# A Fourier mixing layer with a gated MLP: the first stage's four engines ordered by one written list

## The chip, the cores and the metric

The kernel runs on one core of one Trainium2 chip. The core has a matrix engine (TensorE, PE in the profile), a vector engine (VectorE, DVE), a scalar engine (ScalarE, ACT), a general engine (GpSimd, POOL), and DMA queues, most of them issued by SyncE (SP). SBUF is the working memory with 128 partitions; PSUM is the accumulator memory that TensorE writes, with 8 banks of 512 fp32 numbers a partition. POOL here works on SBUF only. Each engine runs its own instruction list in order, and waits where data of another engine is missing. The metric is device time of one execution in microseconds (us); lower is better.

## The reference

```
h  = x + irfft2(rfft2(layernorm(x)) * (w_r + 1j * w_i))
n  = layernorm(h)
h2 = h + (gelu(n @ w_gate) * (n @ w_up)) @ w_down
```

x is 2048 rows of 512 numbers; the filter w is 2048 x 257; the MLP is 1376 wide. All is fp32. layernorm takes mean and variance over the 512 numbers of a row, with 1e-5 added to the variance, and has no weights.

## The kernel before

The rows are cut into 16 blocks b of 128 rows (row 16 p + b lies in partition p), 512 columns each. The Fourier transforms are matrix products with tables. The work runs in stages: a first stage (the transform over the rows within a partition index, block by block), a second stage (the transform over the columns, the filter and the way back, 16 steps t), a third that returns to rows, adds the residual and normalises again, and then the MLP, most of the time. The change touches the first stage only (lines 213 to 400).

For each block b the first stage does this. The letters are those of the written list in the change, and the prediction uses them for both kernels.

- `s`, `g`: bn_stats on DVE over 512 numbers (`stats`, L220) and its merge to mean and variance in `mv` (`merge`, L223). For blocks 5, 7, 9, 11 and 13 ScalarE takes these instead: `m`, the mean by a scaled copy with an accumulator (`mean`, L228), and `q`, the variance by a square with an accumulator (`square`, L233).
- `r`: a reciprocal root of variance + eps on ScalarE (`root`, L240), and beside it on DVE variance + eps into a PSUM tile `tmp` (L241). Blocks 0 and 1 each alone, then pairs (2, 3), (4, 5) and so on.
- `n`: one Newton step on DVE that sharpens the root (`newton`, L246 to L248): three operations, each of which takes one operand from `rs` in SBUF and one from `tmp` in PSUM.
- `c`: the block's 128 x 128 transform matrix times this root on ScalarE (`scale`, L256), from `mfs` into `ms`, so that layernorm's division needs no pass over x.
- `f`: POOL's fold of x: a difference (L262) and a sum (L263) of the two halves of the columns, into `pn`; 256 numbers each for the single blocks 0, 1, 14 and 15, 512 for a pair.
- `v`: the second fold on DVE (`fold2`, L277): the difference of the two halves of `pn`, into `uv`. Both inputs lie in SBUF.
- `u`: the sum that goes with it (L275), into `us`. Before the change it is made for block 15 only.
- `a`, `b`: TensorE's products of the block (`transform`, L288). An fp32 product is two matmul instructions in the trace. Quarters c = 0 and 1 of the output (`a`) take two products each from `pn`, or one each from `us` where `u` was made; quarters 2 and 3 (`b`) take one each from `uv`. So a block is 12 instructions, or 8 with `u`.
- `k`: the copy of the block's PSUM bank (bank b mod 7) on ScalarE into `ts` (`keep`, L293).

The second stage's first matmul (`over_d`, L416) reads `ts` of all 16 blocks.

What sets the order: DVE's instructions of the first stage are issued as the calls stand in the code (`manual_schedule` with DVE alone); the orders of PE, ACT and POOL are made by the framework's planner. In the second and the later stages all four engines follow lists written by hand (`SECOND`, `FIRST`). SP issues the loads in the order of the code: x of blocks 0, 1, 2-3, 4-5, the matrices of blocks 2-7, more x, then tables, the first weights, the filter. `lasts` is the last `fold2`: POOL's work on the first MLP weights (`load_gu(0)`, L138) waits for it (`behind`), to leave DVE the port that both use. ScalarE's halving of `wh` is put behind the last copy, `kept`.

Of the kernel before, what the change touches and what calls it, by code (L numbers as in the profile page):

```python
# [20 lines left out]
P = 128  # L21
NB = 16
# [3 lines left out]
EPS = 1e-5  # L26
# [31 lines left out]
def kernel(  # L58
# [103 lines left out]
    with (  # L162
# [54 lines left out]
        def stats(b):  # L217

            bns[b] = w1.tile([P, 6], F32, name="bn", bufs=4)
            dve.bn_stats(bns[b], gh[:, b])  # L220

        def merge(b):
            dve.bn_aggr(mv[:, b], bns[b])  # L223
# [10 lines left out]


        tmp = ps[:, 7].rearrange("p (b k) -> p b k", b=NB)

        def root(b, n):

            act.activation(rs[:, b : b + n], mv[:, b : b + n, 1], AF.Abs_reciprocal_sqrt, bias=eps)  # L240
            dve.tensor_scalar(tmp[:, b : b + n, 0], mv[:, b : b + n, 1], EPS, None, op0=ALU.add)  # L241

        def newton(b, n):

            r, (ve, t) = rs[:, b : b + n], (tmp[:, b : b + n, k] for k in range(2))
            dve.scalar_tensor_tensor(t, r, -0.5, ve, op0=ALU.mult, op1=ALU.mult)  # L246
            dve.tensor_tensor(t, t, r, op=ALU.mult)
            dve.scalar_tensor_tensor(r, t, 1.5, r, op0=ALU.add, op1=ALU.mult)  # L248

        mss, parts = {}, {}  # L250

        def scale(*bs):

            for b in bs:
                mss[b] = w1.tile([P, 2, P // 2], F32, name="ms", bufs=6)
                act.activation(mss[b], mfs[:, b], AF.Copy, scale=rs[:, b : b + 1])  # L256

        def fold(b, n):
            xv = gh[:, b : b + n].rearrange("p b (e n) -> p b e n", e=2)
            pn = w1.tile([P, 2, 2, 2, P], F32, name="pn", bufs=7)[:, :n]  # L260
            pv = pn.rearrange("p b e h n -> p b e (h n)")
            pool.tensor_tensor(pv[:, :, 1], xv[:, :, 0], xv[:, :, 1], op=ALU.subtract)  # L262
            pool.tensor_tensor(pv[:, :, 0], xv[:, :, 0], xv[:, :, 1], op=ALU.add)  # L263
            for i in range(n):
                parts[b + i] = [[pn[:, i, 0, 0], pn[:, i, 0, 1]], [pn[:, i, 1, 0], pn[:, i, 1, 1]]]
            return pn

        def fold2(b, n, sums=False):

            nonlocal lasts  # L270
            pn = pns[b]
            uv = w1.tile([P, 2, 2, P], F32, name="uv", bufs=3)[:, :n]
            if sums:
                us = w1.tile([P, 2, P], F32, name="us", bufs=1)
                dve.tensor_tensor(us, pn[:, 0, :, 0], pn[:, 0, :, 1], op=ALU.add)  # L275
                parts[b] = [[us[:, 0]], [us[:, 1]]]
            lasts = dve.tensor_tensor(uv, pn[:, :, :, 0], pn[:, :, :, 1], op=ALU.subtract)  # L277
            for i in range(n):
                parts[b + i] += [[uv[:, i, 0]], [uv[:, i, 1]]]

        def transform(b):

            pt = ps[:, b % 7].rearrange("p (c n) -> p c n", c=4)
            for c in range(4):

                mc = mss[b][:, :: -1 if c in (1, 2) else 1]
                for z, o in enumerate(parts[b][c]):
                    pe.matmul(pt[:, c], o, mc, start=(z == 0), stop=(z == len(parts[b][c]) - 1))  # L288

        def keep(b):  # L290
            pt = ps[:, b % 7].rearrange("p (c n) -> p c n", c=4)
            tv = ts[:, :, :, :, b].rearrange("p t c g k -> p t (c g) k")
            return act.activation(tv, pt.rearrange("p c (g t k) -> p t (c g) k", g=2, k=4), AF.Copy)  # L293

        pns = {b: fold(b, n) for b, n in GROUPS}
        with tc.manual_schedule(engines={mybir.EngineType.DVE}):

            stats(0)
            merge(0)
            root(0, 1)  # L300
            stats(1)
            newton(0, 1)
            merge(1)
            root(1, 1)
            fold2(0, 1)
            scale(0)
            newton(1, 1)
            fold2(1, 1)
            mean(5)
            transform(0)  # L310
            keep(0)
            scale(1)
            transform(1)
            keep(1)
            stats(2)
            merge(2)
            stats(3)
            merge(3)
            root(2, 2)
            square(5)  # L320
            stats(4)
            newton(2, 2)
            scale(2, 3)
            merge(4)
            root(4, 2)
            fold2(2, 2)
            transform(2)
            keep(2)
            transform(3)
            keep(3)  # L330
            mean(7)
            square(7)
            stats(6)
            newton(4, 2)
            scale(4, 5)
            merge(6)
            root(6, 2)
            fold2(4, 2)
            transform(4)
            keep(4)  # L340
            transform(5)
            keep(5)
            mean(9)
            square(9)
            stats(8)
            newton(6, 2)
            scale(6, 7)
            merge(8)
            root(8, 2)
            fold2(6, 2)  # L350
            transform(6)
            keep(6)
            transform(7)
            keep(7)
            mean(11)
            square(11)
            stats(10)
            newton(8, 2)
            scale(8, 9)
            merge(10)  # L360
            root(10, 2)
            fold2(8, 2)
            transform(8)
            keep(8)
            transform(9)
            keep(9)
            mean(13)
            square(13)
            stats(12)
            newton(10, 2)  # L370
            scale(10, 11)
            merge(12)
            root(12, 2)
            fold2(10, 2)
            transform(10)
            keep(10)
            transform(11)
            keep(11)
            stats(14)
            newton(12, 2)  # L380
            scale(12, 13)
            merge(14)
            stats(15)
            merge(15)
            root(14, 2)
            fold2(12, 2)
            transform(12)
            keep(12)
            transform(13)
            keep(13)  # L390
            newton(14, 2)
            scale(14, 15)
            fold2(14, 1)
            transform(14)
            keep(14)
            fold2(15, 1, sums=True)
            transform(15)
# [63 lines left out]
        def patch_w(t):  # L461
            act.activation(wts[t][:, :, :, 0:129:128], wh[:, t], AF.Copy)

        et = mybir.EngineType
# [486 lines left out]
        next(begun_tiles[n])  # L951

    do["g2P0"] = lambda: step(2)
    et = mybir.EngineType
# [216 lines left out]
```

## Time and profile before

| | us |
|---|---|
| median of 3 runs (454.14 to 454.22) | 454.15 |
| the profiled execution | 454.05 |
| its span, first to last instruction | 452.3 |
| PE busy | 437.8 (97%) |
| POOL busy | 276.5 (61%) |
| DVE busy | 277.1 (61%) |
| ACT busy | 205.6 (45%) |
| first matmul of the first stage | at 7.28 |
| last copy of the first stage ends | at 32.26 |
| first matmul of the second stage | at 32.30 |

The span runs from the first to the last instruction of the profiled execution; 1.75 us of its time lie outside. A row of the timeline gives start (us), duration (us), engine, line, operation, what it writes and reads, the shape, and in brackets the idle time before it and what ended it. "x8" means eight instructions merged into one row. A row of the chain gives start, length and the engine and line that the end of the kernel hung on. A row of the windows gives a stretch, its length, and busy time (with instruction count) of each engine in the order PE, PE's weight loads, DVE, ACT, POOL, then the granted TensorE clock, the DMA share and GB/s. Instructions of one engine overlap a little: a duration can be longer than the distance to the next start.

### The profile page before, as it was taken

The page shows a single profiled execution, that of the slowest core. Times are in us where ns is not written, and L with a number is a line of the kernel's source. Part 1 is how long each engine was busy: PE and PEld are TensorE (multiplying, and loading weights), DVE is VectorE, ACT ScalarE, POOL GpSimd, SP SyncE. Part 2 cuts the span into 40 slices and gives each one's busy share as a digit, 9 for nine tenths or more (in the row PEclk, how much of TensorE's full clock was granted, in tenths as well). Part 3 has the DMA queues.
Part 4 walks back from the last instruction along what each step waited for, and adds up shares of the span by engine and source line. Part 5 has one row for each costly group of instructions (what it writes and reads, how often), then busy time and mean ns, then how long its engine had stood idle before and what let it go on. Part 6 is the DMA issues. An engine that isn't in the chain of part 4 may idle for free.

```text
span 452.3 us, 6433 instructions
## 1 busy us (share of the span) xinstructions
PE 437.8 (97%) x2289; PEld 371.1 (82%) x2289; DVE 277.1 (61%) x514; ACT 205.6 (45%) x433; POOL 276.5 (61%) x306
## 2 busy tenths in 40 slices
PE   3999999999999999999999999999999999999996
PEld 3999999798878777877888888888888888888875
DVE  5957895797574766358735578266555345635453
ACT  4979785688731242033332765252243034303420
POOL 6986896878859578748662543165566636653210
PEclk9999999999999999999999999999999999999999
DMA  8994805200032022112210213121022102210013
GB/s 288 390 400 147 278 13 179 100 23 1 25 116 93 26 69 93 48 46 71 70 48 23 70 48 116 49 91 46 26 70 71 46 24 71 70 46 25 23 70 118
DMA packets 21168, 41.05 MB, mean 91 GB/s; under 512 B 2064, under 2 KB 7696, under 8 KB 21008
## 3 DMA queue, kind: packets, MB, share of 16 engines
q1 hardware_dynamic: 20992, 40.51, 26.3%
q8 instruction: 18, 0.29, 0.3%
q10 hardware_dynamic: 144, 0.13, 0.1%
q14 instruction: 14, 0.11, 0.1%
HBM read 36.44 MB, written 4.19 MB: 90 GB/s over the span
## 4 chain that ended last, share of the span: by engine, by line
PE 90%; DVE 3%; ACT 2%; DMA 2%; POOL 1%; issue 1%; SPq 0%; POOLq 0%; DVEq 0%
PE ps L756 26%; PE ps L100 15%; PE ps L102 14%; PE ps L101 14%; PE ps L288 4%; PE ps L416 3%; PE ps L427 3%; PE ps L454 3%; PE ps L524 3%; PE ps L862 1%; PE ps L971 1%; DMA gh<-in_x 1%; POOL gu L156 1%; PE ps L563 1%; DMA raw<-in_wgu 1%; PE ps L557 1%
## 5 line engine op out<-in xcount | busy, mean ns | idle before, releaser
L100 PE MATMUL ps<-cb,gu 128*128 128x512 f32 (+1 forms) x336 | 127.9, 381 | 2.0 <-ACT s L660 1.6
L756 PE MATMUL ps<-wd,a 128*128 128x512 f32 (+1 forms) x537 | 125.9, 388 | 0.2 <-DVE gh L759 0.2
L102 PE MATMUL ps<-cb,gu 128*128 128x512 f32 (+1 forms) x336 | 125.0, 372 | 0.0
L101 PE MATMUL ps<-cb,gu 128*128 128x512 f32 (+1 forms) x336 | 124.9, 372 | 0.0
L756 PEld LDWEIGHTS ps<-wd,a 128*128 128x128 f32 x537 | 99.4, 188 | 21.9 <-DVE gh L972 1.0
L156 POOL TENSOR_TENSOR gu<-raw,gu 128x768 fp32r<-128x768 f32 (+1 forms) x54 | 78.3, 1479 | 39.6 <-DVE gu L153 33.4
L660 ACT ACTIVATE s<-ps 128x512 f32<-128x512 f32 (+1 forms) x72 | 40.4, 560 | 133.8 <-PE ps L102 133.5
L100 PEld LDWEIGHTS ps<-cb,gu 128*128 128x128 f32 x336 | 63.3, 188 | 14.9 <-ACT s L660 2.2
L101 PEld LDWEIGHTS ps<-cb,gu 128*128 128x128 f32 x336 | 63.3, 188 | 11.7 <-issue 1.0
L102 PEld LDWEIGHTS ps<-cb,gu 128*128 128x128 f32 x336 | 63.3, 188 | 11.0
L762 DVE TENSOR_TENSOR gh<-ps,gh 128x512 f32<-128x512 f32 x48 | 33.1, 691 | 53.7 <-PE ps L756 53.5
L505 POOL TENSOR_TENSOR wd<-wdr,wd 128x512 fp32r<-128x512 f32 x22 | 28.4, 1291 | 51.3 <-ACT wd L503 51.2
L669 DVE TENSOR_TENSOR ps<-ps,s 128x512 f32<-128x512 f32 (+1 forms) x48 | 31.0, 650 | 24.4 <-PE ps L102 22.2
L675 ACT ACTIVATE a<-ps 128x512 fp32r<-128x512 f32 (+1 forms) x48 | 26.9, 561 | 39.0 <-DVE ps L669 38.6
L682 DVE TENSOR_TENSOR a<-ps,a 128x512 fp32r<-128x512 f32 (+1 forms) x48 | 30.8, 641 | 11.5 <-ACT a L675 9.8
L663 DVE TENSOR_TENSOR s<-ps,s 128x512 f32<-128x512 f32 (+1 forms) x48 | 30.9, 643 | 10.6 <-PE ps L102 9.1
L666 ACT ACTIVATE s<-s 128x512 f32<-128x512 f32 (+1 forms) x48 | 28.2, 592 | 18.4 <-DVE s L663 18.4
L138 POOL TENSOR_TENSOR raw<-raw 128x256 f32<-128x256 f32 x20 | 14.7, 737 | 33.9 <-DMA raw<-in_wgu 32.4
L663 DVE TENSOR_TENSOR ps<-ps,s 128x512 f32<-128x512 f32 (+1 forms) x24 | 15.7, 654 | 27.8 <-ACT s L660 27.8
L288 PE MATMUL ps<-ms,pn 128*128 128x128 f32 x120 | 17.0, 291 | 7.9 <-ACT ms L256 7.8
L288 PEld LDWEIGHTS ps<-ms,pn 128*128 128x128 f32 x120 | 15.6, 205 | 8.3 <-POOL pn L263 7.2
L153 DVE CAST gu<-raw 128x1792 fp32r<-128x1792 f32 x18 | 19.6, 1091 | 3.8 <-PE ps L101 2.9
(126 smaller groups left out, 609.5 us busy)
## 6 DMA issues: line engine op xcount, KB each, us to landing
raw<-in_wgu SPq DMA_DIRECT2D x40, 256.0 KB, 3.1
wt<-in_w SPq DMA_DIRECT2D x16, 520.0 KB, 5.7
wdr<-in_wd SPq DMA_DIRECT2D x22, 256.0 KB, 2.7
out<-gh SPq DMA_DIRECT2D x15, 256.0 KB, 2.0
gh<-in_x SPq DMA_DIRECT2D x7, 512.0 KB, 8.1
row<-in_x SPq DMA_DIRECT2D x12, 256.0 KB, 3.0
mis<-in_mi SPq DMA_DIRECT2D x1, 1024.0 KB, 10.6
a<-in_x SPq DMA_DIRECT2D x4, 256.0 KB, 4.9
```

The source lines that it names most:

```text
L100: pe.matmul(o, lh, rh, start=(i == 0 and not onto), stop=False, skip_group_check=True)
L101: pe.matmul(o, lh, rl, start=False, stop=False, skip_group_check=True)
L102: last = pe.matmul(o, ll, rh, start=False, stop=(i == n - 1), skip_group_check=True)
L156: pooled["lo"] = pool.tensor_tensor(r[:, 1, m], t[:, m], r[:, 0, m].bitcast(F32), op=ALU.subtract)
L288: pe.matmul(pt[:, c], o, mc, start=(z == 0), stop=(z == len(parts[b][c]) - 1))
L505: pool.tensor_tensor(r[:, 1], t, r[:, 0].bitcast(F32), op=ALU.subtract)
L660: return lambda: act.activation(to, a, AF.Copy)
L663: return lambda: dve.tensor_tensor(to, a, b, op=ALU.add)
L669: return lambda: dve.tensor_tensor(u, u, g, op=ALU.mult)
L682: dve.tensor_tensor(a[:, 1], u, a[:, 0].bitcast(F32), op=ALU.subtract)
L756: pe.matmul(o, parts_of[tiles.index((q, f))][:, ha, i // 4, r], wds[f][:, hw, c], start=start, stop=stop)
L762: dve.tensor_tensor(gh[:, b, c], o, gh[:, b, c], op=ALU.add)
```

## The change

The calls of the first stage are replaced by one list, `START`, in which all four engines' steps stand in one order; `manual_schedule` now covers PE, ACT, DVE and POOL, so each engine's order is what the list gives it. Beside this:

- Newton for all but block 0: L241's separate operation is gone. The first of the three operations is now (variance + eps) x r, with the variance from `mv` and r from `rs`, both in SBUF, and its result in PSUM. For block 0 the step is kept with a prepared -0.5 (variance + eps) in PSUM, takes two operations, and its last product is put into the scaling of the matrix, which DVE does (`d0`).
- Mean and square on ScalarE for block 3 too (blocks 3, 5, 7, 9, 11, 13); the slice `odd`, whose means are brought to scale at the end, grows from 5 to 6.
- The block sums `u` on DVE for blocks 11, 13 and 14 beside 15; one operation now makes both sums of a block.
- Quarters 0 and 1 of a block's products (`a`) and quarters 2 and 3 (`b`) are separate steps. The list has them in the order a0 b0 a1 b1 ... a15 b15.
- The last block's copy out of PSUM: quarters 0 and 1 on DVE after a15, quarters 2 and 3 on ScalarE (`k15`).
- `lasts` is now the second fold of block 15 by the list, `kept` the ScalarE copy `k15`, and the last second folds and block sums stand as n14 u14 v14 u15 v15 in DVE's order.

By engine the list reads: DVE s0 g0 r0 s1 v0 g1 n0 d0 s2 n1 g2 s4 n2 g4 v1 v2 n4 s6 s8 v4 g6 s10 n6 g8 v6 s12 n8 g10 g12 v8 s15 n10 s14 g14 v10 u11 n12 g15 v12 u13 n14 u14 v14 u15 v15 and the copy of a15; ACT r0 r1 m3 q3 m5 r2 c1 q5 c2 r4 k0 c3 m7 k1 m9 c4 q7 k2 c5 r6 q9 c6 c7 k3 r8 m11 k4 c8 q11 c9 r10 m13 q13 c10 k5 k6 r12 c11 k7 c12 k8 c13 r14 k9 c14 k10 c15 k11 k12 k13 k14 k15; POOL f0 f1 f2 f4 f6 f8 f10 f12 f14 f15, as before.

```diff
--- before.py
+++ after.py
+START = """
+s0 f0 g0 r0 s1 f1 v0 g1 n0 r1 m3 d0 f2 s2 a0 q3 n1 m5 b0 g2 s4 r2 c1 n2 q5 a1 g4 f4 v1 c2 r4 v2 k0 b1 c3 a2 m7 n4 k1
+b2 s6 a3 m9 s8 f6 c4 v4 b3 q7 a4 k2 g6 s10 c5 b4 r6 q9 a5 n6 g8 f8 c6 v6 b5 c7 k3 a6 r8 m11 s12 b6 k4 a7 n8 g10 c8 g12
+f10 q11 v8 b7 a8 c9 r10 m13 s15 b8 q13 a9 n10 s14 c10 f12 k5 b9 g14 a10 k6 v10 r12 c11 k7 u11 b10 n12 a11 g15 c12 b11
+f14 k8 v12 a12 c13 r14 k9 u13 b12 n14 a13 f15 u14 c14 b13 k10 v14 a14 c15 u15 k11 b14 v15 k12 a15 k13 b15 k14 k15
+"""
...
-
+        group = {b + i: (b, n) for b, n in GROUPS for i in range(n)}
+
+        def root(b):
+
+            n = 1 if b < 2 else 2
             act.activation(rs[:, b : b + n], mv[:, b : b + n, 1], AF.Abs_reciprocal_sqrt, bias=eps)
-            dve.tensor_scalar(tmp[:, b : b + n, 0], mv[:, b : b + n, 1], EPS, None, op0=ALU.add)
-
-        def newton(b, n):
-
-            r, (ve, t) = rs[:, b : b + n], (tmp[:, b : b + n, k] for k in range(2))
-            dve.scalar_tensor_tensor(t, r, -0.5, ve, op0=ALU.mult, op1=ALU.mult)
-            dve.tensor_tensor(t, t, r, op=ALU.mult)
+            if b == 0:
+                dve.tensor_scalar(tmp[:, 0, :1], mv[:, 0, 1:], EPS, -0.5, op0=ALU.add, op1=ALU.mult)
+
+        def newton(b):
+
+            if b == 0:
+                r, ve, t = rs[:, :1], tmp[:, 0, :1], tmp[:, 0, 1:2]
+                dve.tensor_tensor(t, ve, r, op=ALU.mult)
+                dve.tensor_scalar(t, t, r, 1.5, op0=ALU.mult, op1=ALU.add)
+                return
+            n = 1 if b < 2 else 2
+            r, t = rs[:, b : b + n], tmp[:, b : b + n, 0]
+            dve.scalar_tensor_tensor(t, mv[:, b : b + n, 1], EPS, r, op0=ALU.add, op1=ALU.mult)
+            dve.scalar_tensor_tensor(t, t, -0.5, r, op0=ALU.mult, op1=ALU.mult)
             dve.scalar_tensor_tensor(r, t, 1.5, r, op0=ALU.add, op1=ALU.mult)
 
-        mss, parts = {}, {}
-
-        def scale(*bs):
-
-            for b in bs:
-                mss[b] = w1.tile([P, 2, P // 2], F32, name="ms", bufs=6)
-                act.activation(mss[b], mfs[:, b], AF.Copy, scale=rs[:, b : b + 1])
-
-        def fold(b, n):
+        mss, pns, parts = {}, {}, {b: [None] * 4 for b in range(NB)}
+
+        def scaled(b):
+            mss[b] = w1.tile([P, 2, P // 2], F32, name="ms", bufs=6)
+            return mss[b].rearrange("p e n -> p (e n)")
+
+        def scale(b):
+            act.activation(scaled(b), mfs[:, b], AF.Copy, scale=rs[:, b : b + 1])
+
+        def scale0(b):
+            dve.tensor_scalar(scaled(b), mfs[:, b], rs[:, b : b + 1], tmp[:, b, 1:2], op0=ALU.mult, op1=ALU.mult)
+
+        def fold(b):
+            n = group[b][1]
             xv = gh[:, b : b + n].rearrange("p b (e n) -> p b e n", e=2)
-            pn = w1.tile([P, 2, 2, 2, P], F32, name="pn", bufs=7)[:, :n]
+            pn = pns[b] = w1.tile([P, 2, 2, 2, P], F32, name="pn", bufs=7)[:, :n]
             pv = pn.rearrange("p b e h n -> p b e (h n)")
             pool.tensor_tensor(pv[:, :, 1], xv[:, :, 0], xv[:, :, 1], op=ALU.subtract)
             pool.tensor_tensor(pv[:, :, 0], xv[:, :, 0], xv[:, :, 1], op=ALU.add)
             for i in range(n):
-                parts[b + i] = [[pn[:, i, 0, 0], pn[:, i, 0, 1]], [pn[:, i, 1, 0], pn[:, i, 1, 1]]]
-            return pn
-
-        def fold2(b, n, sums=False):
+                parts[b + i][:2] = [[pn[:, i, 0, 0], pn[:, i, 0, 1]], [pn[:, i, 1, 0], pn[:, i, 1, 1]]]
+
+        def fold2(b):
 
             nonlocal lasts
-            pn = pns[b]
+            n, pn = group[b][1], pns[b]
             uv = w1.tile([P, 2, 2, P], F32, name="uv", bufs=3)[:, :n]
-            if sums:
-                us = w1.tile([P, 2, P], F32, name="us", bufs=1)
-                dve.tensor_tensor(us, pn[:, 0, :, 0], pn[:, 0, :, 1], op=ALU.add)
-                parts[b] = [[us[:, 0]], [us[:, 1]]]
             lasts = dve.tensor_tensor(uv, pn[:, :, :, 0], pn[:, :, :, 1], op=ALU.subtract)
             for i in range(n):
-                parts[b + i] += [[uv[:, i, 0]], [uv[:, i, 1]]]
-
-        def transform(b):
+                parts[b + i][2:] = [[uv[:, i, 0]], [uv[:, i, 1]]]
+
+        def sums2(b):
+            pn = pns[group[b][0]][:, b - group[b][0]]
+            us = w1.tile([P, 2, P], F32, name="us", bufs=5)
+            dve.tensor_tensor(us, pn[:, :, 0], pn[:, :, 1], op=ALU.add)
+            parts[b][:2] = [[us[:, 0]], [us[:, 1]]]
+
+        def transform(b, cs):
 
             pt = ps[:, b % 7].rearrange("p (c n) -> p c n", c=4)
-            for c in range(4):
+            for c in cs:
 
                 mc = mss[b][:, :: -1 if c in (1, 2) else 1]
                 for z, o in enumerate(parts[b][c]):
                     pe.matmul(pt[:, c], o, mc, start=(z == 0), stop=(z == len(parts[b][c]) - 1))
 
+        def kept_of(b, c):
+            pt = ps[:, b % 7].rearrange("p (c n) -> p c n", c=4)[:, c]
+            tv = ts[:, :, c, :, b].rearrange("p t c g k -> p t (c g) k")
+            return tv, pt.rearrange("p c (g t k) -> p t (c g) k", g=2, k=4)
+
         def keep(b):
-            pt = ps[:, b % 7].rearrange("p (c n) -> p c n", c=4)
-            tv = ts[:, :, :, :, b].rearrange("p t c g k -> p t (c g) k")
-            return act.activation(tv, pt.rearrange("p c (g t k) -> p t (c g) k", g=2, k=4), AF.Copy)
-
-        pns = {b: fold(b, n) for b, n in GROUPS}
-        with tc.manual_schedule(engines={mybir.EngineType.DVE}):
-
-            stats(0)
-            merge(0)
-            root(0, 1)
...
-            kept = keep(15)
-            odd = slice(5, 14, 2)
+            return act.activation(*kept_of(b, slice(2 if b == NB - 1 else 0, 4)), AF.Copy)
+
+        def by_halves(b):
+            transform(b, (0, 1))
+            if b == NB - 1:
+                dve.tensor_copy(*kept_of(b, slice(0, 2)))
+
+        steps = {
+            "s": stats,
+            "g": merge,
+            "m": mean,
+            "q": square,
+            "r": root,
+            "n": newton,
+            "c": scale,
+            "d": scale0,
+            "f": fold,
+            "v": fold2,
+            "u": sums2,
+            "a": by_halves,
+            "b": lambda b: transform(b, (2, 3)),
+            "k": keep,
+        }
+        et = mybir.EngineType
+        with tc.manual_schedule(engines={et.PE, et.Activation, et.DVE, et.Pool}):
+            for op in START.split():
+                kept = steps[op[0]](int(op[1:]))
+            odd = slice(3, 14, 2)
             dve.tensor_scalar(mv[:, odd, 0], m4[:, odd], -(D**0.5), None, op0=ALU.mult)
```

More of the change, by code (lines that the diff above doesn't have):

```diff
@@ L293, in keep @@
-            return act.activation(tv, pt.rearrange("p c (g t k) -> p t (c g) k", g=2, k=4), AF.Copy)
-        pns = {b: fold(b, n) for b, n in GROUPS}
-        with tc.manual_schedule(engines={mybir.EngineType.DVE}):
-            stats(0)
-            merge(0)
-            root(0, 1)
[L301 to L397, printed above, removed]
-            kept = keep(15)
-            odd = slice(5, 14, 2)
@@ L953 @@
     do["g2P0"] = lambda: step(2)
-    et = mybir.EngineType
     with tc.manual_schedule(engines={et.PE, et.Activation, et.DVE, et.Pool}):
```

2 lines of the change are left out of this document (removed).

## The prediction

> **What bounds the kernel now.** Read first the page's chain of work that ended last, then the same chain in order of time over the first 45 us, since the change lies only there.
>
> ```profile
> PE 90%; DVE 3%; ACT 2%; DMA 2%; POOL 1%; issue 1%; SPq 0%; POOLq 0%; DVEq 0%
> ```
> ```profile
> 12.27 8.61 PE ps L288 x72
> 20.88 0.06 issue
> 20.94 10.70 PE ps L288 x92
> ...
> 31.66 0.61 ACT ts L293
> ...
> 32.30 2.95 PE ps L416 x24
> ```
>
> TensorE carries 90% of the span. The first stage is handed over at one point: the last copy of a block out of PSUM (L293) ends at 32.26 us, and the second stage's first matmul (L416) starts at 32.30. From there TensorE leads with hardly a gap, so I take every us by which that copy moves as one us of the kernel. Before it, TensorE runs almost unbroken from 12.27 to 31.6: the first stage seems bound by its 164 matmuls. The busy time in one stretch of it warns against that reading:
>
> ```profile
> 18.10:21.00 2.90, 2.84 (x25) 2.68 (x24) 2.73 (x8) 2.90 (x10) 2.90 (x3) 1.00 1.08 390
> ```
>
> In 2.9 us DVE is busy 2.73, ACT and POOL 2.90. All four are full, so which one sets the pace must be read instruction by instruction. The timeline, POOL and DVE rows of a little over one pair of blocks:
>
> ```profile
> 14.03 1.27 POOL L263 TENSOR_TENSOR pn<-gh 128x512 f32<-128x512 f32 x1
> 14.30 1.55 DVE L277 TENSOR_TENSOR uv<-pn 128x512 f32<-128x512 f32 x1
> ...
> 15.26 1.73 POOL L262 TENSOR_TENSOR pn<-gh 128x512 f32<-128x512 f32 x1
> ...
> 15.78 0.68 DVE L220 BATCH_NORM_STATS2 bn<-gh 128x6 f32<-128x512 f32 x1
> ...
> 16.38 0.14 DVE L246 SCALAR_TENSOR_TENSOR ps<-rs,ps 128x2 f32<-128x2 f32 x1
> ...
> 16.55 0.17 DVE L247 TENSOR_TENSOR ps<-ps,rs 128x2 f32<-128x2 f32 x1
> 16.76 0.16 DVE L248 SCALAR_TENSOR_TENSOR rs<-ps,rs 128x2 f32<-128x2 f32 x1
> ...
> 16.83 0.17 DVE L223 BATCH_NORM_AGGREGATE mv<-bn 128x2 f32<-128x6 f32 x1
> ...
> 17.11 0.17 DVE L241 TENSOR_SCALAR ps<-mv 128x2 f32<-128x2 f32 x1
> 17.22 1.55 DVE L277 TENSOR_TENSOR uv<-pn 128x512 f32<-128x512 f32 x1
> ...
> 18.69 0.68 DVE L220 BATCH_NORM_STATS2 bn<-gh 128x6 f32<-128x512 f32 x1
> ```
>
> POOL's two folds of a pair (L262, L263) and DVE's second fold (L277) repeat every 2.92 us (14.30 to 17.22), and they stretch one another. Where POOL is idle, half as much of the same DVE work takes 0.42:
>
> ```profile
> 28.18 0.42 DVE L277 TENSOR_TENSOR uv<-pn 128x256 f32<-128x256 f32 x1
> ```
> ```profile
> 11.12 1.26 POOL L263 TENSOR_TENSOR pn<-gh 128x512 f32<-128x512 f32 x1
> ...
> 11.86 1.07 DVE L277 TENSOR_TENSOR uv<-pn 128x512 f32<-128x512 f32 x1
> ```
>
> All rows fit one **waiting rule**. L277 reads two tensors from SBUF; if POOL is inside an instruction, L277 starts 0.14 before that instruction's recorded end and then takes 0.69, and POOL's next one ends 1.14 after L277 does. Check: 15.30 - 0.14 + 0.69 = 15.85, as 14.30 + 1.55; 15.85 + 1.14 = 16.99, as 15.26 + 1.73; and for the other phase 12.38 - 0.14 + 0.69 = 12.93, as 11.86 + 1.07. So DVE waits 0.4 to 0.9 us a pair. It loses little by that: POOL needs 1.27 + 1.73 less two overlaps of 0.04, which is 2.92 a pair, so POOL's folds are the pacemaker and DVE fits one L277 in each pair. DVE's small Newton operations show no such wait (0.14 to 0.17): each has one operand in PSUM. A small operation with both operands in SBUF stands once in the trace, on a tensor of two elements, beside a POOL instruction:
>
> ```profile
> 72.90 0.73 POOL L441 TENSOR_TENSOR z<-t,t 128x260 f32<-128x260 f32 x1
> ```
> ```profile
> 72.93 0.73 DVE L444 TENSOR_TENSOR z<-z 128x2 f32<-128x2 f32 x1
> ```
>
> 0.73 us for 2 elements, ending 0.03 after POOL's: 73.63 - 0.14 + 0.16 = 73.65. Width does not matter, the operands do.
>
> **The change part by part.**
>
> *Newton.* The separate operation var + eps into PSUM (L241, x9) goes, except for block 0. From 16.83 to 17.22 the trace has merge, L241 and the next fold; without L241 about 0.29 a pair falls out of DVE. But the new first operation takes var from `mv` and r from `rs`, both in SBUF, and writes PSUM. No such scalar_tensor_tensor is in the trace. Ends: 0.14 (L246, no wait) and 0.14 plus a whole POOL instruction, 1.13. I take the waiting rule, as its nearest row is the two-element one above. The Trainium skill, SBUF — State Buffer, section "Who interferes with whom", names any Vector instruction with two SBUF inputs as contending with a GpSimd one that reads SBUF; the trace agrees for tensor_tensor, and by that rule the new operation waits as well.
>
> *Start.* DVE now does the second statistics, merge and block 0's second fold ahead of Newton 0, and multiplies block 0's matrix itself (`d0`).
>
> ```profile
> 5.55 0.69 DVE L220 BATCH_NORM_STATS2 bn<-gh 128x6 f32<-128x512 f32 x1 [0.16 <-DMA gh<-in_x]
> ...
> 6.38 0.72 POOL L263 TENSOR_TENSOR pn<-gh 128x256 f32<-128x256 f32 x1
> ...
> 6.74 0.40 ACT L256 ACTIVATE ms<-mfs,rs 128x128 f32<-128x128 f32 x1 [1.21 <-DVE rs L248]
> ...
> 7.06 1.46 POOL L262 TENSOR_TENSOR pn<-gh 128x512 f32<-128x512 f32 x1
> ...
> 7.28 2.05 PE L288 MATMUL ps<-ms,pn 128*128 128x128 f32 x8 [7.28 <-ACT ms L256]
> ...
> 8.47 1.45 POOL L263 TENSOR_TENSOR pn<-gh 128x512 f32<-128x512 f32 x1
> ...
> 9.89 1.26 POOL L262 TENSOR_TENSOR pn<-gh 128x512 f32<-128x512 f32 x1
> ```
>
> Statistics 1 end at 6.24; v0 starts when POOL's first fold of block 1 lets go (6.27) and ends 6.67; the two operations of Newton 0 end at 7.03; `d0` (ends of its cost: 0.17 as L241, or that plus 1.13; I take 0.24 and 0.08 of wait, since POOL's instruction is just ending) 7.37; first matmul 7.5 against 7.28. That costs nothing: TensorE starves until about 12 in any case.
>
> *Middle, walked along the new DVE list.* POOL runs f2 7.23 to 9.74, f4 to 12.39 (held up 0.19 by v1). Statistics 2 end 7.98; Newton 1 waits 0.47 and ends 8.91; statistics 4, Newton 2 to 10.14, merge 4, v1 10.16 to 11.25 (wait 0.67), v2 11.17 to 12.94 (wait 1.08, until 12.25). At 12.94 POOL's f6 goes on, to 14.08. The next in the list is Newton 4, right behind v2: its first operation can't start before 13.94. This is the decisive step. Newton 4 ends 14.48, statistics 6 and 8 follow, v4 is ready at 15.60 and has missed POOL's boundary at 15.31; it goes at the next, 16.40 to 17.09. The trace of before has that fold end at 15.85: 1.24 late. After that the pace is POOL's again: v6 ends 20.01, v8 22.93, v10 25.99, against 18.77 (17.22 + 1.55) for v6 before and 2.92 a pair from there. What the shorter list saves (statistics and merge of block 3, some 0.8; L241s, some 2) is spent waiting for POOL.
>
> *Block sums u11, u13, u14 new (u15 stood before).* Each is 0.42 of DVE, read from two SBUF tensors, and halves 8 matmuls to 4. Weight loads come at 0.111 us ((0.97 - 0.19) / 7):
>
> ```profile
> 29.11 0.97 PEld L288 LDWEIGHTS ps<-ms,pn 128*128 128x128 f32 x8
> ```
>
> so TensorE loses 12 x 0.111 = 1.33 us of work; it is worth that only where TensorE is last. u11 stands ahead of Newton 12: 25.91 to 26.87 with 0.54 of wait; Newton 12 then waits 0.54 and ends 27.86. Before, it ended at 25.66:
>
> ```profile
> 23.40 0.30 ACT L240 ACTIVATE rs<-mv,eps 128x2 f32<-128x2 f32 x1
> 23.59 1.08 ACT L293 ACTIVATE ts<-ps 128x512 f32<-128x512 f32 x2
> ...
> 25.50 0.16 DVE L248 SCALAR_TENSOR_TENSOR rs<-ps,rs 128x2 f32<-128x2 f32 x1
> ...
> 25.70 0.69 ACT L256 ACTIVATE ms<-mfs,rs 128x128 f32<-128x128 f32 x2 [1.03 <-DVE rs L248]
> ```
>
> *ScalarE.* Block 3's mean and square come to it: 0.61 and 0.71 start to start, a scale 0.30, a root 0.18, a copy 0.475:
>
> ```profile
> 18.11 0.72 ACT L233 ACTIVATE jk<-gh,m 128x512 f32<-128x512 f32 x1
> ...
> 18.82 0.59 ACT L293 ACTIVATE ts<-ps 128x512 f32<-128x512 f32 x1
> 19.30 0.63 ACT L228 ACTIVATE jk<-gh 128x512 f32<-128x512 f32 x1
> ```
>
> They lie before 9 us, where ACT had waits (it first waits for `mv`), and cost nothing. If that cover goes, they cost 1.32.
>
> *Tail.* From Newton 12 the ACT list is c12 k8 c13 r14 k9 c14 k10 c15 k11 k12 k13 k14 k15, in order and by the written list: 4 scales 1.20, 7 copies 3.33, the root 0.18, the half copy of block 15 0.35, and 0.24 of waiting for Newton 14 (29.84): 5.30. So 27.89 + 5.30 = 33.19. TensorE's tail (blocks 12 to 15 from 28.41: 12 + 3 x 8 matmuls at 0.111, waits of a third of a us, latency) ends 32.6, and DVE's half of the last copy 32.60; both are covered by ACT. The last copy split saves 0.24 of ACT, counted above.
>
> *Moved with it.* The DMA issues on SP and ACT keep their order; nothing is moved past them. POOL's chain for the first weights waits for the last second fold, which moves from 29.28 to 31.20 us:
>
> ```profile
> 29.36 0.73 POOL L138 TENSOR_TENSOR raw<-raw 128x256 f32<-128x256 f32 x1 [1.11 <-DVE uv L277]
> ...
> 36.46 0.72 POOL L94 TENSOR_TENSOR gu<-raw,gu 128x256 fp32r<-128x256 f32 x1 [2.22 <-ACT gu L93]
> ```
>
> It starts 1.9 later, and the 2.22 idle ahead of the later row takes that up. If that cover were gone, the weights' split would be late, for TensorE not before 80 us. Longer constant `odd`, PE halves: no cost found.
>
> *Sum.* 33.19 - 32.26 = +0.93 on the profiled execution of 454.05 (span 452.3): 454.98. The median of the runs is 0.10 above that execution: 455.1.
>
> **The rivals.** *No wait in Newton (faster side).* If the new operation passes at 0.14, Newton 4 ends 13.40, v4 catches the boundary at 15.30 and ends 15.86 as before; v10 ends 24.62, Newton 12 25.96, the ACT tail 5.4 later 31.36: -0.90, so 453.2. For it: L246's rows; against: the two-element row. It decides from a wait shorter than 0.7 in Newton 4, when v4 is ready by 15.2.
>
> *One boundary more is missed.* u13, Newton 14, u14, v14, u15 and v15 each read SBUF twice; if one operation ahead of Newton 12 comes just behind POOL's start, another 1.13 goes: +2.1, 456.2. For it: DVE now asks for the port 23 times, against 11. Against: the walk lands in mid-instruction mostly.
>
> *The lists do what they say.* Were no operation held by POOL, TensorE would be last: 176 matmuls at 0.111 from 7.5 with the starved 1.6 us, end 28.7: -3.5, 450.6. Against it speaks every L277 row.
>
> **How the numbers follow.** Forecast 0.62, the Newton rival 0.20, a missed boundary 0.13, TensorE-bound 0.05. Within 0.2% means within 0.91 us, about what a measurement of this kernel can tell from no change. The forecast lies on that edge; its walk is good to some 0.5 us, so its own range is 454.5 to 455.7 and half of it counts as slower. Faster: half of 0.20, 0.05 and little else, 0.17; same: nearly half of 0.62 and a little of the Newton rival, 0.33; slower: the rest, 0.50. The range for 8 in 10 goes from the Newton rival (453.1) to the missed boundary (456.3).
>
> **What would show it.** Right: the new first Newton operation has a mean well above 0.3 us, Newton 4's about 1.2; second folds still 2.92 apart and about 1.2 late; ACT without idle from Newton 12 on; L416 at 33.2. Wrong: that operation at 0.15; or L416 before 32; or idle time on ACT in the tail, which would make TensorE or DVE the last; or a gap after 36 us that the second stage did not have.

## The result, and the profile after

The changed kernel takes 455.43 us (median of 8 runs, 455.29 to 455.82); the kernel before takes 454.14 beside it. The ratio is 1.0028 (95% interval 1.0018 to 1.0038): 1.29 us slower. The whole interval lies above 1, and the ratio lies a little beyond the 0.2% up to which the prediction counts a result as the same. The forecast was 455.1. The profiled execution took 455.29 with a span of 453.5; that of before took 454.05, so the traces account for +1.24.

The chain of the changed kernel, in order of time over the first 38 us (start, length, engine, what, line; lines have moved: Newton is L262 to L264, `d0` L276, POOL's folds L283 and L284, `v` L293, `u` L300, the products L310, the last copies L318 and, on DVE, L323, the second stage L362):

```profile
7.17 1.44 DVE ms L276
...
11.50 2.69 DVE uv L293 x2
14.19 1.17 DVE ps L262
...
15.66 1.28 DVE bn L227 x2
16.93 1.41 DVE uv L293
...
18.39 2.05 PE ps L310 x16
...
20.46 5.83 PE ps L310 x48
...
26.32 6.22 PE ps L310 x52
...
32.56 0.44 DVE ts L323
...
33.04 0.71 PE ps L310 x4
33.75 0.45 PE ps L362 x4
...
34.22 2.50 PE ps L362 x20
```

Before, TensorE stood on this chain from 12.27 on. Now VectorE holds it until 18.34: `d0`, the folds v1 and v2, the first operation of Newton 4 (1.17 us of the chain, for 2 elements a partition), two statistics, v4. Then 116 matmuls run without a break, and at the end there is a step that was not there before: the last four matmuls of the first stage wait for VectorE's copy. The second stage's first 24 matmuls follow in two parts, since twenty of them need ScalarE's half copy too; they end at 36.72, where before they ran from 32.30 to 35.25.

The windows show the two parts. Columns: stretch and length, then busy time and count of PE, its weight loads, DVE, ACT and POOL. Before:

```profile
8.70:18.40 9.70, 9.14 (x71) 8.87 (x71) 9.14 (x27) 9.03 (x29) 9.70 (x8) 1.00 1.02 395
18.40:32.50 14.10, 13.35 (x115) 12.91 (x114) 10.41 (x31) 11.32 (x31) 12.75 (x14) 1.00 1.03 403
```

After:

```profile
8.70:18.40 9.70, 8.71 (x57) 8.51 (x57) 9.49 (x20) 6.74 (x20) 9.70 (x8) 1.00 1.02 388
18.40:32.50 14.10, 14.05 (x116) 13.34 (x116) 12.37 (x35) 12.87 (x36) 10.47 (x12) 1.00 1.03 404
```

In the first stretch the changed kernel does 57 matmuls where 71 were done; in the second TensorE is busy 14.05 of 14.10 us. So what was late at 18.4 could not be made up, although 12 matmuls had been taken out. VectorE's operations of the first 34 us grouped by shape (count, busy us, mean ns) name the new wait, the timeline places it:

```profile
L262 DVE SCALAR_TENSOR_TENSOR ps<-mv,rs 128x2 f32<-128x2 f32 x7 | 3.3, 469 | 0.1
L263 DVE SCALAR_TENSOR_TENSOR ps<-ps,rs 128x2 f32<-128x2 f32 x7 | 1.2, 168 | 0.2
```
```profile
6.40 0.90 POOL L284 TENSOR_TENSOR pn<-gh 128x256 f32<-128x256 f32 x1
7.17 1.44 DVE L276 TENSOR_SCALAR ms<-mfs,rs,ps 128x128 f32<-128x128 f32 x1
7.26 1.26 POOL L283 TENSOR_TENSOR pn<-gh 128x512 f32<-128x512 f32 x1
...
13.60 1.72 POOL L284 TENSOR_TENSOR pn<-gh 128x512 f32<-128x512 f32 x1
14.11 1.24 DVE L262 SCALAR_TENSOR_TENSOR ps<-mv,rs 128x2 f32<-128x2 f32 x1
...
16.85 1.48 DVE L293 TENSOR_TENSOR uv<-pn 128x512 f32<-128x512 f32 x1
...
18.39 0.71 PE L310 MATMUL ps<-ms,uv 128*128 128x128 f32 x4 [0.93 <-DVE uv L293]
...
25.95 0.71 DVE L293 TENSOR_TENSOR uv<-pn 128x512 f32<-128x512 f32 x1
...
32.56 0.43 DVE L323 COPY ts<-ps 128x256 f32<-128x256 f32 x1 [1.10 <-PE ps L310]
33.04 0.71 PE L310 MATMUL ps<-ms,uv 128*128 128x128 f32 x4 [0.52 <-DVE ts L323]
...
33.79 0.38 ACT L318 ACTIVATE ts<-ps 128x256 f32<-128x256 f32 x1 [0.51 <-PE ps L310]
```

L262 reads two tensors in SBUF, L263 one in PSUM and one in SBUF; they are of one kind and size, and take 0.469 and 0.168 us. In Newton 4, L262 ends at 15.35, 0.03 after POOL's instruction of 13.60 (end 15.32), the same distance as in the prediction's two-element row.

### The profile page after: what moved, and what is told of

It reads as the page before. It is cut to its first block, busy times and chain, and to the rows that moved or that the text cites. A ratio compares the mean times of both kernels' runs of the same rounds, so it can differ in the third digit from the quotient of the medians.

```text
span 453.5 us, 6396 instructions
## 1 busy us (share of the span) xinstructions
PE 437.3 (96%) x2277; PEld 370.1 (82%) x2277; DVE 280.0 (62%) x508; ACT 206.6 (46%) x436; POOL 276.1 (61%) x306
## 4 chain that ended last, share of the span: by engine, by line
PE 91%; DVE 4%; ACT 2%; DMA 1%; issue 1%; SPq 0%
PE ps L701 26%; PE ps L107 15%; PE ps L108 15%; PE ps L109 15%; PE ps L310 3%; PE ps L362 3%; PE ps L373 3%; PE ps L469 3%; PE ps L400 3%; PE ps L807 1%; PE ps L915 1%; DVE uv L293 1%; DMA gh<-in_x 1%; PE ps L508 1%; PE ps L502 1%
## 5 line engine op out<-in xcount | busy, mean ns | idle before, releaser
L611 ACT ACTIVATE s<-s 128x512 f32<-128x512 f32 (+1 forms) x48 | 28.2, 592 | 18.4 <-DVE s L608 18.4
L310 PE MATMUL ps<-ms,pn 128*128 128x128 f32 x96 | 14.8, 304 | 8.8 <-DVE ms L276 8.8
L310 PEld LDWEIGHTS ps<-ms,pn 128*128 128x128 f32 x96 | 13.3, 215 | 9.3 <-issue 9.3
```

## The experiments

The theory: the first operation of the new Newton step waits for POOL, and through v4 that costs the time. The rivals: the written lists, `d0` or the divided last copy cost it. Every ratio below is to the kernel before, on the same chip in the same job (its median there was 454.04, 454.23 or 454.26).

**The Newton step alone, in the kernel before.** Everything else is as before.

```diff
-            dve.tensor_scalar(tmp[:, b : b + n, 0], mv[:, b : b + n, 1], EPS, None, op0=ALU.add)
...
+            r, t = rs[:, b : b + n], tmp[:, b : b + n, 0]
+            dve.scalar_tensor_tensor(t, mv[:, b : b + n, 1], EPS, r, op0=ALU.add, op1=ALU.mult)
+            dve.scalar_tensor_tensor(t, t, -0.5, r, op0=ALU.mult, op1=ALU.mult)
             dve.scalar_tensor_tensor(r, t, 1.5, r, op0=ALU.add, op1=ALU.mult)
```

> The kernel before, with the three-step Newton of the change alone: its first op reads mv and rs, both in SBUF; the lists, the sums and the last copy stay as they were. The waiting rule: each step's first op waits for a POOL instruction to end, as the 1.24 us of Newton 4 in the changed kernel did; with the 1.2 us that a missed boundary costs there, 455.1 to 455.5 against about 454.1. The rival (one operation fewer a pair is a gain, or Newton lies under cover, and the written lists cost the time): 453.7 to 454.2.

455.40 us (455.07 to 455.82), ratio 1.0027 (1.0017 to 1.0036): as the waiting rule has it. One operation fewer a pair makes the kernel before as slow as the whole change does.

**The same with the root in PSUM.** ScalarE writes the root to `tmp` in PSUM, and Newton's intermediate moves in exchange from PSUM to `nt`, a new tile in SBUF, so that none of the three operations reads two tensors in SBUF. The diff is against the run above.

```diff
-            act.activation(rs[:, b : b + n], mv[:, b : b + n, 1], AF.Abs_reciprocal_sqrt, bias=eps)
+            act.activation(tmp[:, b : b + n, 2], mv[:, b : b + n, 1], AF.Abs_reciprocal_sqrt, bias=eps)
...
-            r, t = rs[:, b : b + n], tmp[:, b : b + n, 0]
+            r, t = tmp[:, b : b + n, 2], nt[:, b : b + n]
...
-            dve.scalar_tensor_tensor(r, t, 1.5, r, op0=ALU.add, op1=ALU.mult)
+            dve.scalar_tensor_tensor(rs[:, b : b + n], t, 1.5, r, op0=ALU.add, op1=ALU.mult)
```

> The same as the run before this one in the list, with the root in PSUM, so that no Newton op reads two tensors in SBUF. The waiting rule: no wait in Newton, and the folds still go by POOL's instructions, 2.92 us a pair: 454.0, within 0.3. The rival (the op taken out of each Newton step is on the path): 0.3 to 1 us faster than before, 453.1 to 453.8.

453.87 us (453.62 to 454.36), ratio 0.9993 (0.9983 to 1.0002): 1.53 us from the run above, with the same operations in the same order, and only the root and the intermediate in other memories. The first Newton operation (minimum, median and maximum in ns, first and last start) in the first of these kernels and in the second:

```profile
L245 DVE SCALAR_TENSOR_TENSOR ps<-mv,rs x9: 146/632/1041, 6.2 to 27.8; 128x2 f32<-128x2 f32 x7, 128x1 f32<-128x1 f32 x2
```
```profile
L246 DVE SCALAR_TENSOR_TENSOR nt<-mv,ps x9: 131/143/157, 6.3 to 26.4; 128x2 f32<-128x2 f32 x7, 128x1 f32<-128x1 f32 x2
```

That the first writes into PSUM is not what makes it wait: in the kernel before, L246 writes there too, and takes 0.15 on average.

**The changed kernel with the root in PSUM**, the same edit for blocks 1 to 15, taken twice on two chips.

> The changed kernel with one thing undone: ScalarE writes the root of blocks 1 to 15 into PSUM (and Newton's intermediate goes to SBUF), so that no Newton operation reads two SBUF tensors; count and order of the operations stay. Waiting rule (an operation with two SBUF operands waits for POOL's instruction in progress): the first Newton operation falls from a mean of 0.47 us to 0.14-0.18, Newton 4 no longer waits (1.24 to 0.15), the last first-stage copy ends some 1.5 us earlier, time 453.4 to 454.4 against 455.4 of the changed kernel. Rival, the new order of the lists and the larger share of ScalarE set the pace: the operation gets short all the same, but DVE or ScalarE waits elsewhere and the time stays at 455.1 to 455.6.

452.86 us (452.62 to 453.9), ratio 0.9979 (0.997 to 0.9988).

> The changed kernel with the root in PSUM once more, as the reference of the two runs beside it: 452.6 to 453.2.

453.23 us (452.77 to 454.22), with the same ratio (0.9969 to 0.9989). The direction is the theory's, the size more than expected: it is 2.2 to 2.6 us below the changed kernel and a us below the one before. So the rest of the change (lists, sums, `d0`, block 3's mean, divided copy) is worth 0.0014 of the time (0.9993 to 0.9979, some 0.6 us, little more than the intervals leave open) beside the short Newton step without its wait, and nothing beside the one that waits (1.0027 and 1.0028). Beside the Newton of before, which does not wait either, it costs 0.0018 (below). So the written lists are no gain in themselves: what they are worth hangs on the Newton step. The chain of the second take of this kernel:

```profile
8.70 21.78 PE ps L312 x172
```

From the first matmul to 30.48 it is TensorE alone. VectorE's waits have left the chain, though most folds of a pair still have them (1.36, 1.04 and 1.71 us in v4, v6 and v10, where v8 and v12 took 0.66 and 0.68).

**Block 0 scaled on ScalarE again** (`c0`), the rest as changed.

```diff
-... n0 r1 m3 d0 f2 ...
+... n0 r1 c0 m3 f2 ...
...
                 dve.tensor_scalar(t, t, r, 1.5, op0=ALU.mult, op1=ALU.add)
+                dve.tensor_tensor(r, t, r, op=ALU.mult)
```

> The changed kernel with block 0's matrix scaled on ScalarE again, as before the change (Newton 0 gets its third operation back; the scale stands ahead of block 3's mean). In the changed kernel DVE's scaling took 1.44 us, as it waited for a whole POOL instruction. Waiting rule: the first matmul starts at 7.7 instead of 8.8, but Newton 1 and 2 then run into the next POOL instructions (waits of about 0.8 and 1.0 in place of 0.5 and 0.1), block 1's second fold ends at the same boundary as before, and the time stays: 455.2 to 455.6. Rival, the 1.1 us at the start carries through to the end: 454.1 to 454.5.

455.32 us (455.08 to 455.41), ratio 1.0026 (1.0014 to 1.0038): no gain. The 1.2 us that `d0` waited are waited in Newton 2 instead, and Newton 4 waits as before:

```profile
9.96 1.13 DVE L263 SCALAR_TENSOR_TENSOR ps<-mv,rs 128x2 f32<-128x2 f32 x1 [0.27 <-ACT rs L249]
...
14.18 1.23 DVE L263 SCALAR_TENSOR_TENSOR ps<-mv,rs 128x2 f32<-128x2 f32 x1
```

**The last copy undivided on ScalarE**, the rest as changed.

```diff
-            return act.activation(*kept_of(b, slice(2 if b == NB - 1 else 0, 4)), AF.Copy)
+            return act.activation(*kept_of(b, slice(0, 4)), AF.Copy)
...
-            if b == NB - 1:
-                dve.tensor_copy(*kept_of(b, slice(0, 2)))
```

> The changed kernel with the last block's copy out of PSUM undivided on ScalarE. In the changed kernel TensorE's last products (block 15, quarters 2 and 3) waited 0.5 us for DVE's copy out of the same bank, and ScalarE waited 0.5 us for them. If that wait is what the split costs: TensorE's last products end at 33.2 instead of 33.7, ScalarE's copy takes 0.6 in place of 0.38 and the second stage starts 0.2 to 0.3 us earlier: 455.0 to 455.3. Rival, the split pays: 455.5 to 455.8.

455.58 us (455.23 to 455.93), ratio 1.0034 (1.0021 to 1.0047): dividing it neither pays nor costs by these runs, since the interval takes in the 1.0028 of the changed kernel. Expected was a gain if TensorE's wait is what the division costs. The wait of 0.52 is gone here too, but then ScalarE's whole copy comes last, and the second stage waits 0.85 us for it.

**All three turned**: root in PSUM, `c0`, undivided copy.

> All three together: root in PSUM, block 0's scaling on ScalarE, last copy undivided. Waiting rule: second fold of blocks 4-5 ends at 15.85 as in the kernel before, those of the next pairs 2.92 us apart; the last copy ends at 32.0 to 32.3, so the time is 453.9 to 454.3, the kernel before's within 0.2 us, since POOL's and DVE's instructions with two SBUF operands share the time of one port and the block sums add to them. Rival, with the waits gone TensorE is last and the twelve matmuls fewer count: last copy at 30.5 to 31, 452.4 to 452.9.

452.84 us (452.43 to 453.2), ratio 0.9974 (0.9965 to 0.9984), a us better than expected. The number is the rival's (452.4 to 452.9), but not for the rival's reason, that TensorE is last: the chain of this run goes over VectorE's folds and block sums to 27.4 and ends with five copies on ScalarE, 28.59 to 31.05. My walk along the list had folds miss boundaries that they caught in the run (v6 started at 17.03 and took 0.66, without a wait).

**The same without the new sums** u11, u13 and u14, struck from the list.

> The version with all three parts turned (452.84 measured) without the three added sums of DVE, u11, u13 and u14, whose blocks TensorE adds up itself with 12 more matmuls. If TensorE is what comes last before the tail, as the prediction's step on the sums has it, the 12 matmuls of 0.111 us put the end 1.0 to 1.3 us later: 453.9 to 454.2. If the sums only take DVE's time ahead of Newton 12 and TensorE has the room, nothing or a gain: 452.5 to 452.8.

454.03 us (453.19 to 455.02), ratio 0.9996 (0.9987 to 1.0006): 0.0022 of the time more by the ratios, 1.0 us for 12 matmuls, as expected if TensorE comes last before the tail. With them TensorE does lead, from its first matmul to 31.91:

```profile
8.14 23.77 PE ps L313 x188
```

**The changed kernel with the Newton of before**, four operations, variance + eps put into PSUM first.

```diff
-            dve.scalar_tensor_tensor(t, mv[:, b : b + n, 1], EPS, r, op0=ALU.add, op1=ALU.mult)
-            dve.scalar_tensor_tensor(t, t, -0.5, r, op0=ALU.mult, op1=ALU.mult)
+            dve.tensor_scalar(tmp[:, b : b + n, 2], mv[:, b : b + n, 1], EPS, None, op0=ALU.add)
+            dve.scalar_tensor_tensor(t, r, -0.5, tmp[:, b : b + n, 2], op0=ALU.mult, op1=ALU.mult)
+            dve.tensor_tensor(t, t, r, op=ALU.mult)
```

> The changed kernel, with its four lists, sums and divided copy, and the four-operation Newton of the kernel before in place of the three-step one. The waiting rule: the waits of Newton go, as with the root in PSUM (452.86 measured), and one short operation of DVE a pair comes back: 452.8 to 453.4. The rival (the lists and the ports set the pace, whatever Newton's form): 455.2 to 455.6, as the changed kernel.

454.97 us (454.89 to 455.71), ratio 1.0018 (1.0008 to 1.0027): a miss. It is between the two expected ranges, 1.7 to 2.1 us above the version with the root in PSUM, though no Newton operation waits. The trace has Newton 2 from 10.61 to 11.43 (four operations), so the extra operation costs 0.3, and it stands twice ahead of v1, which is ready at 11.44 instead of 10.71 and misses a boundary of POOL. I took that for the cause and tried it alone.

**v1 late, nothing else**: the version with the root in PSUM, with the first operation of Newton 2 repeated.

```diff
-            dve.scalar_tensor_tensor(t, mv[:, b : b + n, 1], EPS, r, op0=ALU.add, op1=ALU.mult)
+            for _ in range(5 if b == 2 else 1):
+                dve.scalar_tensor_tensor(t, mv[:, b : b + n, 1], EPS, r, op0=ALU.add, op1=ALU.mult)
```

> The same, with the first operation of Newton 2 issued five times over (it waits for nothing, 0.18 us from one to the next), so that the fold v1 is ready 0.72 us later, at about 11.44 instead of 10.72, as with the old Newton. The theory of the boundary: v1 misses the end of POOL's instruction near 10.9 and waits for the next, 1.23 later, and the folds behind it run late: 454.3 to 455.0. If the old Newton costs by its longer operations throughout and not by v1, this run has only 0.72 us of DVE more, under cover: 452.8 to 453.6.

453.64 us (453.29 to 454.06), ratio 0.9988 (0.9978 to 0.9997); beside it the version without the repeats has 453.23. So the theory of the boundary falls as the price of 1.7 us: v1 did miss it (ready 11.54, v4 ends at 17.10 instead of 15.82), but no matmul waited for that, and v6 was back in step. The folds v4 and v6 and the POOL instruction between them, with the old Newton and then with the late v1:

```profile
16.11 1.07 DVE L294 TENSOR_TENSOR uv<-pn 128x512 f32<-128x512 f32 x1
...
16.60 1.72 POOL L285 TENSOR_TENSOR pn<-gh 128x512 f32<-128x512 f32 x1
...
18.59 1.50 DVE L294 TENSOR_TENSOR uv<-pn 128x512 f32<-128x512 f32 x1
```
```profile
15.75 1.35 DVE L296 TENSOR_TENSOR uv<-pn 128x512 f32<-128x512 f32 x1
...
16.52 1.71 POOL L287 TENSOR_TENSOR pn<-gh 128x512 f32<-128x512 f32 x1
...
18.22 0.66 DVE L296 TENSOR_TENSOR uv<-pn 128x512 f32<-128x512 f32 x1
```

POOL's instructions end at 18.32 and 18.23. With the short Newton v6 is ready at that moment and passes in 0.66; with the old one it is ready 0.27 too late and takes 1.50, and so does v8 (21.50, 1.50); v10 takes 0.98. What VectorE does between v4 and v6 takes 1.12 with the short Newton (17.10 to 18.22) and 1.41 with the old one (17.18 to 18.59), and the POOL instruction ends 1.13 and 1.14 after v4. So the missed boundary is made good where the work between two folds fits into that, and stays where it does not. That the longer Newton operations after v1 cost the remaining 1.3 us is read from these two traces; it was not tried alone. The wait does not account for this run: with the old Newton, which has none, the rest of the change is slower than the kernel before, and why is argued here, not shown.

**Two banks for the last block**: root in PSUM, `c0`, the copy divided as in the change, but quarters 2 and 3 of block 15 in the next PSUM bank.

```diff
             for c in cs:
+                pt = ps[:, (b + (b == NB - 1 and c > 1)) % 7].rearrange("p (c n) -> p c n", c=4)
...
-            pt = ps[:, b % 7].rearrange("p (c n) -> p c n", c=4)[:, c]
+            pt = ps[:, (b + (b == NB - 1 and c.start > 1)) % 7].rearrange("p (c n) -> p c n", c=4)[:, c]
```

> The version with root in PSUM and block 0 scaled on ACT, last copy divided as in the change, but block 15's second half computed into another PSUM bank than its first. If TensorE's wait of 0.52 before the last four matmuls is for DVE's copy out of the same bank, that wait is gone from the trace, and the end, otherwise set by ACT's last copies (30.9 in the undivided version), comes 0.2 to 0.3 us sooner: 452.4 to 452.7. If the wait is not the bank's, it stays, and the time is 452.8 to 453.2.

452.47 us (452.33 to 452.51, 5 runs), ratio 0.996 (0.9947 to 0.9974): as expected, and the best of all. TensorE's last products of the first stage and the start of the second, and ScalarE's last copies:

```profile
29.23 0.68 PE L313 MATMUL ps<-ms,us 128*128 128x128 f32 x4
29.75 0.61 PE L313 MATMUL ps<-ms,uv 128*128 128x128 f32 x4
30.55 2.95 PE L365 MATMUL ps<-dfs,ts 128*128 128x130 f32 x24 [0.19 <-ACT ts L321]
```
```profile
28.45 2.33 ACT L321 ACTIVATE ts<-ps 128x512 f32<-128x512 f32 x5
```

The wait of 0.52 ahead of the last four matmuls is gone, and the wait of the second stage for ScalarE is 0.19. The interval touches that of the version with all three turned (0.9965 to 0.9984), so how much of the time the second bank is worth is not shown. There, with the copy undivided, the start of the second stage had waited 0.69:

```profile
31.10 2.95 PE L363 MATMUL ps<-dfs,ts 128*128 128x130 f32 x24 [0.69 <-ACT ts L321]
```

## Why the prediction was right, and where its steps were off

*One handover point.* Right. The end of the second stage's first 24 matmuls against the time of the same execution:

| | end, us | time, us | difference |
|---|---|---|---|
| before | 35.25 | 454.05 | 418.80 |
| changed | 36.72 | 455.29 | 418.57 |
| Newton alone | 36.60 | 455.16 | 418.56 |
| Newton alone, root in PSUM | 35.17 | 453.80 | 418.63 |
| old Newton | 36.26 | 454.95 | 418.69 |
| all three turned | 34.05 | 452.61 | 418.56 |
| two banks | 33.50 | 452.33 | 418.83 |

The end moves by 3.2 us and the difference stays within 0.27. Of the changed kernel's +1.47 at this point, 0.23 is given back later. The last copy, which the forecast had in this place, went from 32.26 to 34.17; that it ended 1.91 later cost only 1.47, because four of the 24 matmuls now run ahead of it.

*The waiting rule and the new Newton operation.* Right, and it decides the sign. The mean was to be well above 0.3 us: 0.469. Newton 4's was to be about 1.2, behind v2: 1.24. That it is where the operands lie and not the operation: 1.53 us between two kernels that differ only in the places of the root and the intermediate. The Trainium skill, SBUF — State Buffer, section "Who interferes with whom", names any Vector instruction with two SBUF inputs; the runs show this for a scalar_tensor_tensor of two elements a partition too.

*`d0`, taken at 0.24 and 0.08 of wait.* Wrong: 1.44. I had it ready at 7.03 with POOL's instruction just ending. It was ready at 7.17, 0.13 before the recorded end of POOL's row (7.30), and did not get in. It waited for the next, as the rule has it (8.52 - 0.14 + 0.24 = 8.62; measured 8.61), and took a little more than the upper end that the prediction named (0.17 + 1.13). Why it missed the first of these ends is open: the fold v6 of the run with the late v1 started 0.01 before POOL's row ended (18.22 and 18.23) and passed in 0.66, so being there 0.14 ahead is not what all operations need. The first matmul came at 8.76, not 7.5. "That costs nothing" held in its result: without `d0` the changed kernel is no faster (455.32), as Newton 2 waits in its place.

*v4 at 17.09, and from there POOL's pace.* The mechanism right, one boundary more missed: v1 was ready 1.25 later than forecast, and v4 ended at 18.33. A boundary more is what I had put aside as a rival at 456.2, though there for an operation ahead of Newton 12. It did not cost its 1.13. By the chain TensorE leads from 18.39 on, no longer the folds, and the folds caught up: v6 21.24, v8 24.15, v10 26.66, which is 1.23, 1.22 and 0.67 behind the forecast, since the last POOL folds are half as long and v10 passed in 0.71. Newton 12 ended at 28.13, for 27.86 forecast.

*The tail by ScalarE, 33.19.* Wrong in what comes last. After v4 TensorE had no gap that matters (14.05 of 14.10 us), and ScalarE waited for it 0.51. "DVE's half of the last copy is covered by ACT" is the step that failed: TensorE's last products stood behind that copy for 0.52, because both use one PSUM bank; in two banks the wait is gone (whether the chip or only the program's own order asks for it is not shown). Idle time on ScalarE in the tail was one of the prediction's own signs of being wrong, and it came. The last copy ended 0.98 after the forecast. For the whole the forecast had +0.93 on the profiled execution and it was +1.24: of the 0.98, 0.44 did not count because four matmuls of the second stage ran ahead of the copy, and 0.23 was given back later. Neither was foreseen, so that the number came so near is in part luck.

*The sums.* Right as put: worth it where TensorE is last. (One operation made both sums of block 15 in the kernel before, too; that is not new.) That was the case after 18.4, and in the version without waits they are worth 1.0 us.

*The additional mean and square on ScalarE.* In the changed kernel no cost was found, and they were not undone alone. In the version with two banks that cover is gone: VectorE waits 1.18 us for the root, which stands in ScalarE's list behind them and the mean of block 5.

```profile
10.20 0.16 DVE L265 SCALAR_TENSOR_TENSOR nt<-mv,ps 128x2 f32<-128x2 f32 x1 [1.18 <-ACT ps L251]
```

*The first weights on POOL.* Right. They start 2.2 us later (1.9 forecast), and idle time takes that up:

```profile
31.54 0.73 POOL L145 TENSOR_TENSOR raw<-raw 128x256 f32<-128x256 f32 x1 [3.55 <-DVE uv L293]
...
37.93 0.73 POOL L101 TENSOR_TENSOR gu<-raw,gu 128x256 fp32r<-128x256 f32 x1 [1.77 <-ACT gu L100]
```

*The rivals.* "No wait in Newton", 453.2, is what the runs with the root in PSUM made true: 452.86 and 453.23. "The lists do what they say", 450.6, left out when TensorE starts and at what rate: with VectorE off the chain TensorE is last, but from 8.7, and slow at first (below).

## What to carry to other kernels

Count, for each small VectorE operation, how many of its inputs lie in SBUF while GpSimd is busy: here an operation saved was lost, and more, since the one that remained took both from there, and moving one of them to PSUM gave 1.5 us. A wait that ends at another engine's boundaries makes a 0.1 us error of a walk into 1.2 us, but here it was made good where the work between two such operations fitted ahead of the next boundary; so ask what lies between them, and what the next engine has in stock, before adding boundaries up. When a copy out of PSUM is divided between engines to start earlier, give the parts different banks.

## What the runs showed of the hardware

- A tensor_scalar on VectorE, 128x128 from SBUF to SBUF with scalars of a partition, waits for GpSimd as well. In the changed kernel, the one with the root in PSUM and the one with the old Newton it started at 7.17, 7.43 and 7.26 and ended at 8.61, 8.57 and 8.69, each 0.08 or 0.09 after the end of POOL's fold (8.52, 8.48, 8.61). Beside the tensor it reads two scalars of a partition, one in SBUF (`rs`) and one in PSUM; the runs do not separate whether the scalar in SBUF has a part in the wait. The Trainium skill, in the section named above, lists tensor_scalar among the operations that can take the shared ports by a two-port mode, which fits.
- The first matmuls of the execution run at half rate, for a time that differs between executions of one kernel; where TensorE is last, that carries through the stage. The root-in-PSUM kernel started its matmuls at 8.72 and 8.70 in two executions; these are its rows of the first execution and of the second:

```profile
13.12 1.06 PE L312 MATMUL ps<-ms,uv 128*128 128x128 f32 x4
13.97 1.44 PE L312 MATMUL ps<-ms,pn 128*128 128x128 f32 x8
```
```profile
13.10 0.84 PE L312 MATMUL ps<-ms,uv 128*128 128x128 f32 x4
13.78 1.06 PE L312 MATMUL ps<-ms,pn 128*128 128x128 f32 x8
```

  Four matmuls start to start take 0.85 in the first and 0.68 in the second, against 0.45 later; the first goes on slowly for more than 5.2 us and leaves the stage 0.58 behind the second (32.11 and 31.53 at the start of the next; the whole executions took 453.9 and 453.43). The granted clock of these rows' windows reads 1.00 throughout, so it does not show this. The Trainium skill, TensorE: Matmul & The Clock Gate, section "Part 1: The HAM clock gate (the "warmup" mystery)", has a half-rate start of about 3.4 us by a free-running window, different from run to run; the variation agrees, the length here is more. That the range of this kernel's times (452.62 to 453.9 and 452.77 to 454.22) comes from it was not tried.
